# Attention on one core: TensorE's order laid out anew, dummy and bias matmuls taken out, one spare PSUM bank

## The chip, the core and the metric

The kernel runs on one core of one Trainium2 chip. The metric is the device time of one execution in microseconds (us). Executions come in states; where nothing else is said, runs of the same state are compared. Ratios with an interval are the mean time of one kernel's fast runs over that of the other's of the same rounds, so they are not quite the ratio of the medians that are quoted.

## The reference

One attention block in bf16: S = 2048 positions, D = 448, 16 heads of 28.

```
qkv = (x @ wqkv) -> q, k, v            # (16 heads, 2048, 28) each
p   = softmax(q @ k.T * 28 ** -0.5)    # 16 x 2048 x 2048
out = (p @ v, heads side by side) @ wo
```

## The kernel before

The work is cut into 16 units: 4 groups of 4 heads times 4 chunks of 512 queries. A unit has 64 tiles (16 key blocks times 4 heads) of 128 x 512 scores. Most tiles are exponentiated by ScalarE, two or three to an instruction; 109 of the 1024 go to VectorE, which computes the exponential in five instructions. TensorE makes the scores (row-packed, one head in each quarter of the rows), then PV, the product of probabilities and V (column-packed, four heads side by side), the projections of later head groups ("jobs", 38 of them after the start: K, Q and V for one group and one chunk), and the output projection. A block of TensorE writes into a PSUM bank; the instruction that copies it out and frees the bank is its eviction. All orders are static: a list scheduler in the program lays out each engine's instructions from estimated durations.

The parts that the change touches, with cuts marked by "...":

```
LATE0, LATE1 = 1, 8            # units 0 | 1..7 | 8..15 are phases 0 | 1 | 2
def width():                    # ScalarE tiles in one score group
    return ((2, 2), (3, 2), (3, 3))[phase(cur[0])][k % 2]
P.pool("J", [5, 6])             # spare PSUM banks of phases 0 and 1
P.pool("M", [6])                # the spare bank of phase 2
...
def job(...):                   # a projection: 4 TensorE steps, one eviction
    op = P.add("pe", ..., dur=dur, prio=prio, acq=((..."J", 1) if k == 0 else None))
...
def proj_qk(t, g, c, ...):      # K or Q
    if it == 0:                 # constants for VectorE's exponential, in row 28 of each head
        e.matmul(bank(b), CW[:, t, :], ONR[:, :], start=True, stop=False)   # 1 row x 128 columns
    for h in range(4):
        e.matmul(ps[32*h:32*h + DH, ...], w_raw[0:IT, it, col:col + DH], xT[...], start=False, ...)
todo = [(0.85 + (LATE1 - 2.0) * i / len(order),) + o for i, o in enumerate(order)]   # 6.3 jobs a unit
...
# a ScalarE group
s  = P.add("pe", s_mm(... 3 heads ...), dur=330, prio=pr - 5)
ex = P.add("act", exp, ...)
if ph == 2:                     # dummy block: zeros into the open accumulator
    P.add("pe", f_dum, ..., prio=pr + 0.02)
# a VectorE tile: scores of one head, 29 rows
s = P.add("pe", s_mm(... 1 head, DH + 1 rows ...), dur=300, prio=pr - 14/64, acq=("M" or "J", 1))
```

## Time and profile before

| | |
|---|---|
| time, median of 4 runs | 519.11 us (515.7 to 534.44) |
| the profiled run | span 530.0 us, a slow one |
| TensorE, ScalarE, VectorE busy | 92%, 82%, 71% of the span |
| unit 0; units 1 to 6; units 7 to 15; rest | 69.2; 201.6; 242.4; 16.7 us |

From the page of the kernel before: TensorE's busy tenths and its granted clock in 40 slices of the span, then the chain of work that ended last, by engine.

```profile
PE   5999999999999999999999987999799999878884
PEclk9999999985555555555555598557855576999895
...
PE 65%; ACT 31%; DMA 1%; DVE 1%; issue 0%; ACTq 0%
```

TensorE's share of this chain is the largest.

The clock row must be read with care. It shows full clock in the first slices, but the first clock record of this trace is at 87.5 us; before it the row shows 1.0 for want of a record. The timeline of the same kernel (start, duration, engine, line, tile, count), TensorE only:

```profile
30.74 0.61 PE L688 MATMUL ps<-QT,KT 28*128 28x512 bf16 x2
...
31.28 0.61 PE L420 MATMUL ps<-xT,w_raw 112*28 112x512 bf16 x4
...
31.68 0.64 PE L637 MATMUL ps<-PT,V 128*32 128x512 bf16 x4
...
32.25 0.60 PE L688 MATMUL ps<-QT,KT 28*128 28x512 bf16 x2
```

Matmuls packed side by side in the array count as one block. From 31.28 to 31.68 is one column-packed block after another, 0.40 us; from 30.74 to 31.28 there is also a change from row-packed to column-packed, 0.54 us. At half clock over the whole trace a block takes 0.40 to 0.43 us and a change adds 0.10 to 0.14; at full clock a block takes 0.22 us or so and a change adds about 0.10. The start of this run is at half clock.

Windows between the evictions of the accumulator (one a unit; columns: stretch, its length, busy time and count for TensorE, weight loads, VectorE, ScalarE, GpSimd, then granted clock, DMA share, GB/s) for units 3, 7 and 9:

```profile
127.40:164.50 37.10, 37.10 (x250) 9.73 (x247) 27.71 (x50) 28.79 (x25) 0.00 (x0) 0.50 0.04 9
...
270.80:299.70 28.90, 26.08 (x147) 5.07 (x146) 26.41 (x49) 27.88 (x25) 0.00 (x0) 0.50 0.03 11
...
324.60:355.40 30.80, 29.57 (x197) 4.90 (x198) 25.28 (x47) 27.25 (x20) 0.00 (x0) 0.53 0.04 11
```

Unit 3, with projections, is bound by TensorE at half clock: it is busy all of 37.1 us. Unit 7 has no projections and only three dummy blocks, at its end, and is bound by ScalarE. Unit 9 has dummies, and TensorE binds again. The groups that the change removes, from the list by shape:

```profile
L661 PE MATMUL ps<-ZM,ZW 128*32 128x512 bf16 x540 | 65.4, 486 | 0.0
...
L417 PE MATMUL ps<-ONR,CW 1*128 1x512 bf16 x32 | 18.7, 584 | 0.2 <-DMA w_raw<-in_wqkv_dram 0.2
```

### The profile page before, as it was taken

Reading aid. Unit: us, or ns where it says so; the run is one execution under the profiler, and the core shown is the slowest. Engines: PE = TensorE matmul, PEld = TensorE weight load, DVE = VectorE, ACT = ScalarE, POOL = GpSimd, SP = SyncE. Lnnn points to the kernel's source line nnn. Section 1 sums busy time; section 2 is a strip of 40 time slices with the busy share of each in tenths; the row PEclk is TensorE's granted clock in tenths of the full one; section 3 lists DMA queues with packets and bytes.
Section 4 is the critical chain, followed back from the end, with each engine's and each line's share of the span. In section 5 each row is a group of like instructions: output and inputs, shape, how many; then the busy total and the mean of one; then the engine's idle time right before and its main releaser. Section 6 shows DMA issues by size and latency. Waiting matters only on the chain.

```text
span 530.0 us, 8358 instructions
## 1 busy us (share of the span) xinstructions
PE 486.9 (92%) x3557; PEld 118.6 (22%) x3557; DVE 376.8 (71%) x679; ACT 433.9 (82%) x349; POOL 3.9 (1%) x11
## 2 busy tenths in 40 slices
PE   5999999999999999999999987999799999878884
PEld 2442122221222212222111121111111111212131
DVE  2321658996767647666699899879987989594731
ACT  2666678997877768767799999889998999999960
POOL 2000000000000000000000000000000000000000
PEclk9999999985555555555555598557855576999895
DMA  8000000000000000001000000000000000101011
GB/s 258 1 1 0 2 11 15 3 21 2 22 0 3 22 0 23 1 0 23 0 4 20 2 22 3 20 2 22 1 22 1 24 0 24 36 23 36 23 35 41
DMA packets 13843, 10.18 MB, mean 19 GB/s; under 512 B 5932, under 2 KB 11820, under 8 KB 13800
## 3 DMA queue, kind: packets, MB, share of 16 engines
q1 hardware_dynamic: 12872, 8.78, 5.9%
q10 hardware_dynamic: 928, 0.80, 0.5%
q8 instruction: 30, 0.49, 0.4%
q14 instruction: 13, 0.11, 0.1%
HBM read 7.50 MB, written 2.08 MB: 18 GB/s over the span
## 4 chain that ended last, share of the span: by engine, by line
PE 65%; ACT 31%; DMA 1%; DVE 1%; issue 0%; ACTq 0%
ACT PT L700 31%; PE ps L688 26%; PE ps L637 13%; PE ps L420 11%; PE ps L661 6%; PE ps L437 4%; PE ps L417 2%; DMA w_raw<-in_wqkv_dram 1%; PE ps L550 1%; PE ps L401 1%; DVE OTS L573 0%; DVE OUTS L562 0%; PE ps L605 0%; ACT OUTS L560 0%; PE ps L583 0%
## 5 line engine op out<-in xcount | busy, mean ns | idle before, releaser
L700 ACT ACTIVATE PT<-ps 128x1536 bf16<-128x1536 f32 (+1 forms) x343 | 429.7, 1351 | 70.7 <-PE ps L688 67.1
L688 PE MATMUL ps<-QT,KT 28*128 28x512 bf16 (+1 forms) x1024 | 219.2, 532 | 28.9 <-ACT PT L700 26.1
L637 PE MATMUL ps<-PT,V 128*32 128x512 bf16 x915 | 131.9, 540 | 0.0
L718 DVE TENSOR_SCALAR DT<-ps 128x512 int32<-128x512 f32 x109 | 74.7, 685 | 23.6 <-PE ps L688 23.0
L688 PEld LDWEIGHTS ps<-QT,KT 28*128 28x128 bf16 (+1 forms) x1024 | 39.9, 97 | 219.7 <-ACT PT L700 109.2
L722 DVE SCALAR_TENSOR_TENSOR DW<-DW 128x512 f32<-128x512 f32 x109 | 74.2, 683 | 0.9
L724 DVE SCALAR_TENSOR_TENSOR DW<-DW 128x512 f32<-128x512 f32 x109 | 74.1, 682 | 0.4
L726 DVE SCALAR_TENSOR_TENSOR PD<-DT,DW 128x512 int16<-128x512 int32 x109 | 73.5, 677 | 0.8 <-PE ps L637 0.7
L420 PE MATMUL ps<-xT,w_raw 112*28 112x512 bf16 x512 | 65.7, 592 | 0.0
L661 PE MATMUL ps<-ZM,ZW 128*32 128x512 bf16 x540 | 65.4, 486 | 0.0
L637 PE MATMUL ps<-PD,V 128*32 128x512 bf16 x109 | 57.3, 529 | 0.0
L720 DVE TENSOR_SCALAR DW<-DT 128x512 f32<-128x512 uint16 x109 | 45.4, 419 | 0.6
L637 PEld LDWEIGHTS ps<-PT,V 128*32 128x32 bf16 x915 | 26.1, 104 | 49.4 <-issue 44.9
L390 DVE CAST KT<-ps 128x512 bf16<-128x512 f32 x16 | 11.1, 691 | 30.8 <-PE ps L420 30.6
L388 DVE TENSOR_SCALAR QT<-ps 128x512 bf16<-128x512 f32 x15 | 10.3, 688 | 25.2 <-PE ps L420 25.2
L437 PE MATMUL ps<-w_raw,xT 112*128 112x112 bf16 x256 | 28.0, 281 | 0.0
L390 DVE CAST V<-ps 128x448 bf16<-128x448 f32 x16 | 9.9, 622 | 21.0 <-PE ps L437 21.0
L661 PEld LDWEIGHTS ps<-ZM,ZW 128*32 128x32 bf16 x540 | 13.7, 97 | 49.2 <-issue 49.2
L437 PEld LDWEIGHTS ps<-w_raw,xT 112*128 112x128 bf16 x256 | 20.2, 131 | 14.0 <-issue 11.2
L562 DVE CAST OUTS<-ps 128x448 bf16<-128x448 f32 x14 | 8.7, 623 | 20.1 <-PE ps L550 20.1
L550 PE MATMUL ps<-wop,OTN 128*128 128x448 bf16 x64 | 18.5, 406 | 2.4 <-DVE OTN L618 0.8
L420 PEld LDWEIGHTS ps<-xT,w_raw 112*28 112x28 bf16 x512 | 11.7, 107 | 39.4 <-issue 39.1
(44 smaller groups left out, 103.8 us busy)
## 6 DMA issues: line engine op xcount, KB each, us to landing
RB<-scr_r SPq DMA_DIRECT2D x60, 64.0 KB, 2.0
x_nat<-in_x_dram SPq DMA_DIRECT2D x4, 448.0 KB, 7.7
out_dram<-OUTS SPq DMA_DIRECT2D x16, 112.0 KB, 1.7
w_raw<-in_wqkv_dram ACTq DMA_DIRECT2D x2, 392.0 KB, 6.6
w_raw<-in_wqkv_dram SPq DMA_DIRECT2D x1, 392.0 KB, 9.1
wop<-in_wo_dram SPq DMA_DIRECT2D x16, 24.5 KB
scr_l<-OTS SPq DMA_DIRECT2D x15, 8.0 KB
LT<-scr_l SPq DMA_DIRECT2D x15, 8.0 KB, 1.6
```

The source lines that it names most:

```text
L420: ins = e.matmul(ps[32 * h:32 * h + DH, b * 512:(b + 1) * 512], w_raw[0:IT, it, col:col + DH], xT[0:IT, it, c * 512:(c + 1) * 512], start= ...
L437: ins = e.matmul(ps[:, b * 512 + j * GD:b * 512 + (j + 1) * GD], xT[0:IT, it, n * 128:(n + 1) * 128], w_raw[0:IT, it, 2 * D + g * GD:2 * D ...
L550: return e.matmul(bank(hold[0].banks[0])[:, 0:D], OTN[:, gg, n * 128:(n + 1) * 128], wop[:, gg, :], start=(gg == 0), stop=(gg == G - 1))
L637: ins = e.matmul(ps[32 * h:32 * h + 32, ACC * 512:(ACC + 1) * 512], V[:, kt, hh * 32:(hh + 1) * 32], p_ap, start=(kt == 0), stop=(kt == NK ...
L661: ins = e.matmul(ps[32 * h:32 * h + 32, ACC * 512:(ACC + 1) * 512], ZW[:, :], ZM[:, :], start=False, stop=False, skip_group_check=True, ti ...
L688: ins = e.matmul(bank(b), KT[32 * h:32 * h + rows, g, kt * 128:(kt + 1) * 128], QT[32 * h:32 * h + rows, g, c * QCH:(c + 1) * QCH], start= ...
L700: ex = P.add("act", (lambda e, p0=p0, w=w, b0=b0: e.activation(PT[:, p0 * 512:(p0 + w) * 512], bank(b0, w), AF.Exp, scale=ESCALE)), deps=[ ...
L718: o1 = P.add("dve", (lambda e, T=T, s=s: e.tensor_scalar(T, bank(s.banks[0]), 0.0, 255.0 * 65536.0 - 1.0, ALU.max, ALU.min)), deps=[s, d_l ...
L720: o2 = P.add("dve", (lambda e, F16=F16, W=W: e.tensor_scalar(W, F16, ES, EC, ALU.mult, ALU.add)), deps=[o1, d_last[di]], dur=360, prio=pr, ...
L722: o3 = P.add("dve", (lambda e, W=W: e.scalar_tensor_tensor(W, W, EA, W, ALU.add, ALU.mult)), deps=[o2], dur=610, prio=pr, name=f"D3_{gi}")
L724: o4 = P.add("dve", (lambda e, W=W: e.scalar_tensor_tensor(W, W, EB, W, ALU.add, ALU.mult)), deps=[o3], dur=610, prio=pr, name=f"D4_{gi}")
L726: o5 = P.add("dve", (lambda e, W=W, T=T, pi=pi: e.scalar_tensor_tensor(PD[:, pi, :], T, 1.0 / 512.0, W, ALU.mult, ALU.add)), deps=[o4, slo ...
```

## The change

The intent: since TensorE runs at half clock most of the time, lay its order out for that. In parts:

- **Dummies** (540 matmuls, units 8 to 15) go.
- **Bias rows** go. The constants of VectorE's exponential move into its own arithmetic.
- **Riding**: the scores of a VectorE tile are to follow a score group of the three other heads at once, so that all four run together.
- **One spare bank and groups of three** from unit 1 on (from unit 8 on before).
- **Jobs**: at 4.1 a unit by priority instead of 6.3; once begun a job isn't interrupted (priority -4), and its eviction goes first on VectorE.
- **Layout**: the scheduler's durations for TensorE are those of half clock after 45 us, with a price for a change of packing.

```
-    LATE0, LATE1 = 1, 8
+    LATE0, LATE1 = 1, 1
+    def pe_dur(self, prev, op, t):
+        one, switch = (220.0, 100.0) if t < self.FULL_CLOCK_UNTIL else (430.0, 110.0)
+        if prev is None or prev.kind != op.kind:
+            return switch + one * op.units
+        if op.kind == "r" and op.heads and not set(op.heads) & set(prev.heads):
+            return 60.0
+        return one * op.units
...
 def job(...):
-                           dur=dur, prio=prio, ...
+                           kind=kind, units=units_, prio=prio if (k == 0 or early) else -4.0, ...
-            ev = P.add(evac_eng, fe, ..., prio=prio, ...)
+            ev = P.add(evac_eng, fe, ..., prio=prio if early else -100.0, ...)
...
-                    if it == 0:
-                        e.matmul(bank(b), CW[:, t, :], ONR[:, :], start=True, stop=False)
-            todo = [(0.85 + (LATE1 - 2.0) * i / len(order),) + o ...]
+            todo = [(0.85 + i / 4.1,) + o ...]
...
-                if ph == 2:
-                    P.add("pe", f_dum, deps=[ms_zw, ms_zm], after=[s], dur=300, ...)
...
-                s = P.add("pe", ..., deps=deps, dur=300, prio=pr, ...)
+                for j in range(idx[0] - 1 - DLEAD, ..., -1):
+                    if j in s_of and (j - idx[0] + 1) % 4 == 0:
+                        partner, p_pr = s_of[j]
+                        break
+                s = P.add("pe", ..., deps=deps, after=[partner], kind="r", ..., prio=p_pr + 0.0001, ...)
...
+        P.FULL_CLOCK_UNTIL = 45000.0
```

The rule for which tiles go to VectorE changes a little too (114 instead of 109). The diff has two more edits: VectorE's first step of a tile, which frees the spare bank, goes ahead of its other work (priority -90), and K and Q blocks write 32 instead of 28 columns a head.

More of the change, by code (lines that the diff above doesn't have):

```diff
@@ L20 @@
     __slots__ = ("eng", "emit", "deps", "after", "dur", "prio", "name", "idx", "sig", "count",
-                 "t0", "t1", "dma_group", "dma_index", "acq", "rel", "banks", "slack", "nbytes", "relpool", "acq_slack")
+                 "t0", "t1", "dma_group", "dma_index", "acq", "rel", "banks", "slack", "nbytes", "relpool", "acq_slack", "kind", "units", "heads")
     def __init__(self, eng, emit, deps, after, dur, prio, name, idx, dma_group):
@@ L44, in __init__ @@
         self.acq_slack = 0.0
+        self.kind = None
+        self.units = 0.0
+        self.heads = ()
 class _DmaGroup:
@@ L63 @@
     BIGLOOK = 150.0
+    FULL_CLOCK_UNTIL = 0.0
     def __init__(self):
@@ L71, in pool, with add @@
         self.pools[name] = {b: [0.0, None, False] for b in banks}
-    def add(self, eng, emit, deps=(), after=(), dur=100.0, prio=0.0, name="", dma_group=None, acq=None, rel=(), slack=0.0, nbytes=0, acq_slack=0.0):
+    def add(self, eng, emit, deps=(), after=(), dur=100.0, prio=0.0, name="", dma_group=None, acq=None, rel=(), slack=0.0, nbytes=0, acq_slack=0.0, kind=None, units=1.0, heads=()):
         assert dma_group is not None or eng != "sp"
@@ L82, in add @@
         op.acq_slack = acq_slack
+        op.kind = kind
+        op.units = units
+        op.heads = heads
         self.ops.append(op)
         return op
+    def pe_dur(self, prev, op, t):
+        if op.kind is None:
+            return op.dur
+        one, switch = (220.0, 100.0) if t < self.FULL_CLOCK_UNTIL else (430.0, 110.0)
[4 more added lines that the diff above has]
+        return one * op.units
     def schedule(self):
@@ L145, in schedule @@
             op.t0 = st
+            if e == "pe":
+                op.dur = self.pe_dur(order[e][-1] if order[e] else None, op, st)
             op.t1 = st + op.dur
@@ L236 @@
 LOG2E = 1.4426950408889634
-ES = 1.3267265379831447e-05
-EC = 0.0001429470584999315
-EA = 6.764643559880514
-EB = -6.640897709782045
+ES = 3.285997142359445e-05
+EC = 27.848949706562973
+EA = -77.30729786983042
+EB = 1961.0831047043987
+ZLO = -127.0 * 65536.0
+ZHI = 128.0 * 65536.0 - 1.0
 def _fast(nc, x, wqkv, wo, out, n_heads=16):
@@ L265, in _fast @@
     VONE = DH
-    CROW = DH
     QSCALE = 65536.0 * LOG2E * scale
     ESCALE = 1.0 / (65536.0 * LOG2E)
-    KCONST = 127.0
-    QCONST = 3.671875
     assert DH * H == D and G * 4 == H and DH + 1 <= 32 and NIT * IT == D and GD <= IT
@@ L296, in _fast @@
         DW = sb("DW", [128, NDB, 512], FP32)
-        CW = sb("CW", [1, 2, 128], BF16)
-        ONR = sb("ONR", [1, 512], BF16)
+        DU = sb("DU", [128, NDB, 512], FP32)
         OTS = sb("OTS", [128, 2, 512], FP32)
@@ L349, in _fast @@
         ms_wop = P.add("pool", lambda e: e.memset(i32v(wop.rearrange("p g d -> p (g d)")), 0), dur=900, prio=-8, name="ms_wop")
-        CW4 = CW.rearrange("p t (h r) -> p t h r", r=32)
-        ms_c0 = P.add("dve", lambda e: e.memset(CW[:, :, :], 0.0), dur=100, prio=-11, name="ms_c0")
-        ms_cq = P.add("dve", lambda e: e.memset(CW4[:, 0, :, CROW], QCONST), deps=[ms_c0], dur=100, prio=-11, name="ms_cq")
-        ms_ck = P.add("dve", lambda e: e.memset(CW4[:, 1, :, CROW], KCONST), deps=[ms_c0], dur=100, prio=-11, name="ms_ck")
-        ms_onr = P.add("dve", lambda e: e.memset(ONR[:, :], 1.0), dur=100, prio=-11, name="ms_onr")
         ms_one = P.add("pool", lambda e: e.memset(ONE[:, :], 1.0), dur=100, prio=-7, name="ms_one")
@@ L372, in _fast @@
         mid_ev = []
+        cur_pool = ["J"]
         def job(name, prio, mm_ops, evac, early, evac_eng="dve", evac_dur=610, after=(), mul=None):
@@ L377, in job @@
             prev = None
-            for k, (f, deps, dur) in enumerate(mm_ops):
+            pool = "E" if early else cur_pool[0]
+            for k, (f, deps, kind, units_) in enumerate(mm_ops):
                 op = P.add("pe", (lambda e, f=f: f(e, hold[0].banks[0])),
-                           deps=list(deps) + (list(early_ev) if (k == 0 and not early) else []), after=[prev] + list(after),
-                           dur=dur, prio=prio, name=f"{name}_{k}", acq=(("E" if early else "J", 1) if k == 0 else None), acq_slack=0.0 if early else ASLACK)
+                           deps=list(deps) + (list(mid_ev if pool == "M" else early_ev) if (k == 0 and not early) else []), after=[prev] + list(after),
+                           kind=kind, units=units_, prio=prio if (k == 0 or early) else -4.0, name=f"{name}_{k}", acq=((pool, 1) if k == 0 else None), acq_slack=0.0 if early else ASLACK)
                 if k == 0:
@@ L390, in job @@
                 fe = (lambda e: e.tensor_copy(evac[0](), evac[1](hold[0].banks[0])))
-            ev = P.add(evac_eng, fe, deps=[prev] + list(evac[2:]), dur=evac_dur, prio=prio, name=f"{name}_ev", rel=[(hold[0], 0)])
-            (early_ev if early else mid_ev).append(ev)
+            ev = P.add(evac_eng, fe, deps=[prev] + list(evac[2:]), dur=evac_dur, prio=prio if early else -100.0, name=f"{name}_ev", rel=[(hold[0], 0)])
+            if pool != "M":
+                (early_ev if early else mid_ev).append(ev)
             return ev
@@ L403, in f @@
                 return ins
-            xt_ev[(it, n0 // 4)] = job(f"xT{it}_{n0}", prio, [(f, [id_b_op, dma_x[n0 // 4]], 300)],
+            xt_ev[(it, n0 // 4)] = job(f"xT{it}_{n0}", prio, [(f, [id_b_op, dma_x[n0 // 4]], "f", 1.1)],
                                        ((lambda: xT[0:IT, it, n0 * 128:(n0 + 4) * 128]), (lambda b: bank_bf(b)[0:IT, 0:512])),
@@ L415, in f @@
                     ins = None
-                    if it == 0:
-                        e.matmul(bank(b), CW[:, t, :], ONR[:, :], start=True, stop=False)
                     for h in range(4):
                         col = t * D + g * GD + h * DH
-                        ins = e.matmul(ps[32 * h:32 * h + DH, b * 512:(b + 1) * 512], w_raw[0:IT, it, col:col + DH],
-                                       xT[0:IT, it, c * 512:(c + 1) * 512], start=False, stop=(it == NIT - 1), tile_position=(0, 32 * h))
+                        ins = e.matmul(ps[32 * h:32 * h + 32, b * 512:(b + 1) * 512], w_raw[0:IT, it, col:col + 32],
+                                       xT[0:IT, it, c * 512:(c + 1) * 512], start=(it == 0), stop=(it == NIT - 1), tile_position=(0, 32 * h))
                     return ins
-                mms.append((f, [xt_ev[(it, c)]] + ([dma_w[t], ms_cq, ms_ck, ms_onr] if it == 0 else []), 540 if it == 0 else 290))
+                mms.append((f, [xt_ev[(it, c)]] + ([dma_w[t]] if it == 0 else []), "c", 1.0))
             kq_ev[(t, g, c)] = job(f"p{t}_{g}_{c}", prio, mms,
@@ L439, in f @@
                     return ins
-                mms.append((f, [xt_ev[(it, c)] for it in range(NIT)] + [dma_w[2]], 300))
+                mms.append((f, [xt_ev[(it, c)] for it in range(NIT)] + [dma_w[2]], "f", 1.1))
             Vd = V[:, 4 * c:4 * c + 4, g * 128:(g + 1) * 128].rearrange("p n (h r) -> p n h r", r=32)[:, :, :, 0:DH]
@@ L464, in late_jobs, with make_late @@
                 order += [("q", g, c) for c in range(1, NCH)]
-            todo = [(0.85 + (LATE1 - 2.0) * i / len(order),) + o for i, o in enumerate(order)]
-            for pr, kind, g, c in sorted(todo):
+            todo = [(0.85 + i / 4.1,) + o for i, o in enumerate(order)]
+            return sorted(todo)
+        def make_late(jobs):
+            for pr, kind, g, c in jobs:
                 if kind == "v":
@@ L470, in late_jobs @@
                     proj_qk(1 if kind == "k" else 0, g, c, pr, False)
-            return [t[0] for t in todo]
-        late_units = [min(max(int(pr), 0), NU - 1) for pr in late_jobs()]
+        todo_late = late_jobs()
+        late_units = [min(max(int(t[0]), 0), NU - 1) for t in todo_late]
+        make_late([t for t in todo_late if t[0] < LATE1 - 0.25])
         tiles = [(u, kt, h) for u in range(NU) for kt in range(NK) for h in range(4)]
@@ L483, in _fast @@
         on_dve = set()
+        run = 0
         for i, (u, kt, h) in enumerate(tiles):
             if i % 64 == 0:
-                t_d = max(t_d, t_a) + dve_load[u]
-            if t_d + DCOST <= t_a + LEAD and i < NT - 12:
-                t_d = max(t_d, t_a - 2.0) + DCOST
+                t_d += dve_load[u]
+            if t_d + DCOST <= t_a + LEAD and i < NT - 12 and run % (2 if u < LATE0 else 3) == 0:
+                run = 0
+                t_d = max(t_d, t_a - 6.0) + DCOST
                 on_dve.add(i)
@@ L491, in _fast @@
                 t_a += ACOST
+                run += 1
         items = []
@@ L552, in out_proj @@
                 opm = P.add("pe", f_op, deps=[otn_ev[(gg, cc)]] + mid_ev + (([otn_ev[(g_, cc)] for g_ in range(G)] + dma_wo[-1:]) if gg == 0 else []),
-                            after=[prev], dur=260, prio=pr, name=f"OP{n}_{gg}", acq=(("M", 1) if gg == 0 else None), acq_slack=ASLACK)
+                            after=[prev], kind="f", units=0.9, prio=pr if gg == 0 else -4.0, name=f"OP{n}_{gg}", acq=(("M", 1) if gg == 0 else None), acq_slack=ASLACK)
                 prev = opm
@@ L631, in f_pv @@
                 ins = None
-                acc_open[0] = kt != NK - 1
                 for h in range(4):
@@ L641, in pv @@
                        + [v_ev[(g, kt // 4)]] + ([acc_ev[0]] if kt == 0 else []),
-                       after=[last_pv[0]], dur=320, prio=u + (kt + 4) / NK, name=f"PV{u}_{kt}", slack=1200.0 if kt == 0 else 0.0)
+                       after=[last_pv[0]], kind="c", units=1.0, prio=u + (kt + 4) / NK, name=f"PV{u}_{kt}", slack=1200.0 if kt == 0 else 0.0)
             last_pv[0] = op
@@ L650, in _fast @@
         pv_next = 0
-        acc_open = [False]
-        ZW = sb("ZW", [128, 32], BF16)
-        ZM = sb("ZM", [128, 512], BF16)
-        ms_zw = P.add("pool", lambda e: e.memset(ZW[:, :], 0.0), dur=100, prio=-4, name="ms_zw")
-        ms_zm = P.add("pool", lambda e: e.memset(ZM[:, :], 0.0), dur=300, prio=-4, name="ms_zm")
-        def f_dum(e):
-            ins = None
-            if acc_open[0]:
-                for h in range(4):
-                    ins = e.matmul(ps[32 * h:32 * h + 32, ACC * 512:(ACC + 1) * 512], ZW[:, :], ZM[:, :],
-                                   start=False, stop=False, skip_group_check=True, tile_position=(0, 32 * h))
-            return ins
+        s_of = {}
+        DLEAD = 12
         nd = 0
@@ L675, in _fast @@
             ph = phase(idx[0])
+            if ph == 2 and cur_pool[0] != "M":
+                cur_pool[0] = "M"
+                make_late([t for t in todo_late if t[0] >= LATE1 - 0.25])
             if ph > 0 or kind == "D":
@@ L680, in _fast @@
             pr = idx[0] / 64.0 - 0.2
-            rows = DH if kind == "A" else DH + 1
             hold = []
@@ L697, in _fast @@
                 s = P.add("pe", (lambda e, tl=tl, b0=b0: s_mm(e, tl, range(b0, b0 + 3), DH)), deps=deps, after=[last_s[0]],
-                          dur=330, prio=pr - 5, name=f"S{gi}")
+                          kind="r", units=1.0, heads=tuple(h for _, _, h in tl), prio=pr - 5, name=f"S{gi}")
                 last_s[0] = s
+                s_of[idx[-1]] = (s, pr - 5)
                 ex = P.add("act", (lambda e, p0=p0, w=w, b0=b0: e.activation(PT[:, p0 * 512:(p0 + w) * 512], bank(b0, w), AF.Exp, scale=ESCALE)),
@@ L702, in _fast @@
                 last_exp[0] = ex
-                if ph == 2:
-                    P.add("pe", f_dum, deps=[ms_zw, ms_zm], after=[s], dur=300, prio=pr + 0.02, name=f"DUM{gi}")
                 for j, t in enumerate(tl):
@@ L709, in _fast @@
             else:
-                pr -= 14 / 64.0
+                partner, p_pr = None, pr - 14 / 64.0
+                for j in range(idx[0] - 1 - DLEAD, max(idx[0] - 1 - DLEAD - 32, 0), -1):
+                    if j in s_of and (j - idx[0] + 1) % 4 == 0:
+                        partner, p_pr = s_of[j]
+                        break
                 di, pi = nd % NDB, nd % NPD
                 nd += 1
-                s = P.add("pe", (lambda e, tl=tl, hold=hold: s_mm(e, tl, [hold[0].banks[0]], DH + 1)), deps=deps,
-                          dur=300, prio=pr, name=f"SD{gi}", acq=("M" if ph == 2 else "J", 1), acq_slack=ASLACK)
+                s = P.add("pe", (lambda e, tl=tl, hold=hold: s_mm(e, tl, [hold[0].banks[0]], DH)), deps=deps, after=[partner],
+                          kind="r", units=1.0, heads=(tl[0][2],), prio=p_pr + 0.0001, name=f"SD{gi}", acq=("M" if ph == 2 else "J", 1), acq_slack=ASLACK)
@@ L715, in _fast @@
                 hold.append(s)
-                T, W = DT[:, di, :], DW[:, di, :]
+                T, W, U = DT[:, di, :], DW[:, di, :], DU[:, di, :]
                 F16 = DT[:, di, :].bitcast(U16).rearrange("p (n two) -> p n two", two=2)[:, :, 0]
-                o1 = P.add("dve", (lambda e, T=T, s=s: e.tensor_scalar(T, bank(s.banks[0]), 0.0, 255.0 * 65536.0 - 1.0, ALU.max, ALU.min)),
-                           deps=[s, d_last[di]], dur=610, prio=pr, name=f"D1_{gi}", rel=[(s, 0)])
+                o1 = P.add("dve", (lambda e, T=T, s=s: e.tensor_scalar(T, bank(s.banks[0]), ZLO, ZHI, ALU.max, ALU.min)),
+                           deps=[s, d_last[di]], dur=610, prio=-90.0, name=f"D1_{gi}", rel=[(s, 0)])
@@ L720, in _fast @@
                 o2 = P.add("dve", (lambda e, F16=F16, W=W: e.tensor_scalar(W, F16, ES, EC, ALU.mult, ALU.add)),
                            deps=[o1, d_last[di]], dur=360, prio=pr, name=f"D2_{gi}")
-                o3 = P.add("dve", (lambda e, W=W: e.scalar_tensor_tensor(W, W, EA, W, ALU.add, ALU.mult)),
+                o3 = P.add("dve", (lambda e, W=W, U=U: e.scalar_tensor_tensor(U, W, EA, W, ALU.add, ALU.mult)),
                            deps=[o2], dur=610, prio=pr, name=f"D3_{gi}")
-                o4 = P.add("dve", (lambda e, W=W: e.scalar_tensor_tensor(W, W, EB, W, ALU.add, ALU.mult)),
+                o4 = P.add("dve", (lambda e, W=W, U=U: e.scalar_tensor_tensor(U, U, EB, W, ALU.add, ALU.mult)),
@@ L725, in _fast @@
                            deps=[o3], dur=610, prio=pr, name=f"D4_{gi}")
-                o5 = P.add("dve", (lambda e, W=W, T=T, pi=pi: e.scalar_tensor_tensor(PD[:, pi, :], T, 1.0 / 512.0, W, ALU.mult, ALU.add)),
+                o5 = P.add("dve", (lambda e, U=U, T=T, pi=pi: e.scalar_tensor_tensor(PD[:, pi, :], T, 1.0 / 512.0, U, ALU.mult, ALU.add)),
                            deps=[o4, slot_last.get(("D", pi))], dur=610, prio=pr, name=f"D5_{gi}")
```

## The prediction

> **What bounds the kernel now.** TensorE in most of the span, ScalarE's exponentials in the rest: the chain of waits that ended last is 65% TensorE, 31% ScalarE. By stage (windows between the accumulator evictions to OTS): unit 0 ends at 69.2 us; units 1 to 6 take 29.2, 29.0, 37.1, 35.1, 39.0, 32.2 us; units 7 to 14 take 24 to 25 us where the granted clock is mostly full and 30.7 where it is half; the tail takes 16.7 us. The profiled run is a slow one (530; median 518).
>
> The clock lane overstates the clock: its first record is at 87.5 us, yet from 10 to 85 us the timeline shows blocks of four packed matmuls 0.43 us apart, as in the half-clock stages (0.23 to 0.33 at full clock). So TensorE is at half clock before 87.5 us, and from 115 to 306 us. The Trainium skill (TensorE: Matmul & The Clock Gate, "Back-to-back issue gap") gives N/1.2 ns at half clock, 427 ns for 512 columns: the trace agrees. Going from a row-packed block to a column-packed one costs 0.10 us more in the timeline (0.96 us for two blocks and the change); the skill (TensorEngine Tiling (Array Packing), "Key Properties") says that a mode change drains.
>
> A half-clock unit in phase 2 is then 19 score blocks, 8 separate VectorE-tile score blocks, 19 dummy blocks, 16 PV blocks, 62 x 0.43, plus 38 changes x 0.11: 30.9 us; 30.7 measured.
>
> **What the change does**
> - Dummies go (540 matmuls, 135 blocks of 0.43 us at half clock): critical only where the clock is half in units 8 to 15.
> - Bias rows go: 32 matmuls with their mode changes, about 0.54 us each; 6 in unit 0.
> - VectorE-tile scores ride. By the diff's rule for the tile lists, of 114 such tiles (109 before) 65 have a partner group that already holds their head and still cost 0.43; about 46 cost 0.06. Saving 15 to 20 us of TensorE time.
> - Groups of three from unit 1 on: 19 instead of 23 groups per unit, 4 x (0.43 + 0.2) us less on TensorE in units 1 to 7; ScalarE 0.449 us per tile instead of 0.46.
> - Projections spread over units 1 to 9, about 4 jobs per unit instead of 6 to 7, 1.75 us each, uninterrupted; one spare bank serves VectorE tiles, projections and output projections.
>
> **After, per unit at half clock.** Without projections: (19 + 16) x 0.43 + 2 + 4 = 21 us TensorE, below ScalarE's 57 x 0.449 = 25.6. With 4 jobs: 28.5 TensorE; an uninterrupted job delays the next scores, costing ScalarE 0.4 to 1.1 us. VectorE needs about 24.7. All three are near balance: I expect 28.7 us in units 1 to 9 and 26 to 27.5 in units 10 to 14.
>
> Sum: 65.5 + 9 x 28.7 + 5 x 26.5 + 23.5 + 16 = 496; full-clock spells take off a few: 494 us, range 480 to 510. Faster by over 2%: 0.8; within: 0.18; slower: 0.02.
>
> **Right if** no unit takes over 31 us, ScalarE's exponentials take over half of the chain, no ZM/ZW group remains, half clock covers more of the span and matters less, and runs scatter less. **Wrong if** the single spare bank binds (score blocks waiting on VectorE's DT eviction or on copies of K, Q, V), if VectorE's tiles arrive late at PV, or if the clock without dummies behaves differently (much more full clock: 475 to 480).

## More of the kernel before

ScalarE waited 67 us in all for scores (who waited for whom: us in total, times, longest):

```profile
ACT PT L700 <- PE ps L688: 67.1, 96, 2.2
```

## The result, and the profile after

| | before | after |
|---|---|---|
| median of 4 runs | 519.11 us | 470.55 us (458.68 to 481.83) |
| ratio of the fast runs | | 0.8887, 95% interval 0.8812 to 0.8961 |

The kernel is faster by 11%, the prediction said 5%. (Five later rounds on another chip gave 0.8988, so 10%.) The runs of the kernel after are of two kinds: 458.7, 460.5 and 461.8 us, and 479.3 and 481.8. The median lies between them; no run took it. The profile is of the second kind. A later run of the same kernel, unchanged, gave a profile of the first kind (`a_same5` below). Slow beside slow, 530.0 against 477.6; the fast profile has 460.9. The clock row and the chain, first of the profile, then of the fast one:

```profile
PEclk9655555566565657777555758555667756575985
...
ACT 41%; PE 40%; DVE 12%; DMA 4%; issue 2%; SPq 0%; ACTq 0%
```

```profile
PEclk9999556756756577675658695555757555567795
...
ACT 52%; PE 32%; DVE 11%; DMA 2%; issue 1%; SPq 0%
```

ScalarE now leads the chain (31% before), and waits for scores 26 us in all instead of 67 (13 in the fast profile):

```profile
ACT PT L711 <- PE ps L698: 26.1, 54, 1.4
PEld ps L698 <- DVE DT L731: 25.5, 47, 1.1
```

The second line shows the one bank: weight loads for scores that wait until VectorE's DT step frees it (7.3 us in the kernel before). Such idle time is not by itself a loss. VectorE's share of the chain rose from 1% to 12%. The two kinds differ at the start: in the slow one the trace has full clock for one spell of 3.4 us at 11.5 us, then half clock to 104 us; in the fast one full clock from 10.4 to 48 us. Unit 0, first of the slow profile, then of the fast one followed by units 3, 8, 10 and 15:

```profile
0.00:61.50 61.50, 53.48 (x380) 19.38 (x380) 19.81 (x37) 37.65 (x38) 3.43 (x9) 0.62 0.20 55
```

```profile
0.00:44.00 44.00, 35.40 (x380) 15.18 (x380) 19.42 (x38) 34.18 (x38) 3.43 (x9) 1.00 0.26 77
...
99.10:127.00 27.90, 22.76 (x182) 6.94 (x180) 24.25 (x45) 27.18 (x21) 0.00 (x0) 0.68 0.06 12
...
231.60:259.40 27.80, 24.45 (x197) 6.58 (x194) 26.62 (x47) 26.70 (x21) 0.00 (x0) 0.68 0.05 12
...
281.80:306.30 24.50, 22.82 (x145) 5.58 (x143) 24.49 (x47) 24.33 (x19) 0.00 (x0) 0.50 0.04 12
...
415.20:444.10 28.90, 24.37 (x154) 6.85 (x151) 14.18 (x27) 21.45 (x17) 0.00 (x0) 0.80 0.15 50
```

Unit 0 is 17.5 us shorter with the fast start, which is the whole difference between the two profiles (16.7 us). In units 3, 8 and 10 ScalarE is busy over 95% of the time, in unit 10 at a clock of 0.50. Unit 15 is long: in it, ScalarE is busy 21.5 of 28.9 us while output projections run.

Where the time went, with the blocks counted from the starts of the matmuls in both slow traces:

| units 1 to 6 | before | after |
|---|---|---|
| score blocks / PV blocks / K,Q blocks / bias blocks | 164 / 96 / 96 / 24 | 172 / 96 / 48 / 0 |
| V matmuls (about 0.10 us) | 192 | 80 |
| changes of packing (mode changes) | 302 | 169 |
| sum at half clock: blocks x 0.43 + V x 0.10 + changes x 0.11 | 216 us | 162 us |
| measured; ScalarE busy | 201.6; 159.9 us | 162.2; 156.8 us |

The half-clock sum is an estimate from durations of these traces. It fell by 54 us: 32 for jobs moved away, 10 for the bias, 15 for the changes, and 3 back for more score blocks. It counts the bias too dear: of the 24 bias blocks 16 follow a score block without the cost of a change (0.40 us from start to start), and 7 of these start within 0.1 us of it and cost nothing; some 5 of the 216 us are not there. The rest of the gap to 201.6 is in line with the 27 us of full clock from 87.5 us on. The time fell by 39 us, to where ScalarE stands. In units 7 to 15 the 135 dummy blocks went and half of the jobs came: 242.4 to 236.3 us. So most of the gain, 39 of 52 us, lies in units 1 to 6. Riding hardly took place: score blocks are 436 before and 444 after in the whole trace, and in the slow trace after only 19 blocks have four matmuls (12 before). The timeline of the fast profile after, TensorE only, shows why:

```profile
118.64 0.39 PE L698 MATMUL ps<-QT,KT 28*128 28x512 bf16 x3 [0.87 <-ACT PT L711]
118.96 0.40 PE L657 MATMUL ps<-PT,V 128*32 128x512 bf16 x4
119.30 0.39 PE L698 MATMUL ps<-QT,KT 28*128 28x512 bf16 x1
119.98 0.39 PE L698 MATMUL ps<-QT,KT 28*128 28x512 bf16 x3 [0.30 <-ACT PT L711]
...
122.25 0.81 PE L698 MATMUL ps<-QT,KT 28*128 28x512 bf16 x4
```

At 119.30 a VectorE tile's score stands alone, after PV; at 122.25 four matmuls in a row take 0.81 us, not the 0.39 of one block: they didn't all run together. The first started at 122.25, when a DT step had freed the bank, the other three at 122.67. By the order of TensorE's instructions, 81 of the 114 follow a PV block. By the scheduler's own times (its order made again from the kernel), the one spare bank, for which they wait, is still held when the partner's score block ends in 79 of the 114, mostly by the VectorE tile before.

### The profile page after: what moved, and what is told of

Same layout as the page of the kernel before. It is cut to its first block, busy times and chain, and to the rows that moved or that the text cites. A ratio compares the mean times of both kernels' runs of the same rounds, so it can differ in the third digit from the quotient of the medians.

```text
span 477.6 us, 7257 instructions
## 1 busy us (share of the span) xinstructions
PE 418.7 (88%) x2985; PEld 113.1 (24%) x2985; DVE 387.9 (81%) x700; ACT 419.8 (88%) x321; POOL 3.4 (1%) x9
## 4 chain that ended last, share of the span: by engine, by line
ACT 41%; PE 40%; DVE 12%; DMA 4%; issue 2%; SPq 0%; ACTq 0%
ACT PT L711 41%; PE ps L698 16%; PE ps L657 8%; PE ps L434 8%; PE ps L451 4%; PE ps L571 3%; DVE DT L731 3%; DVE DU L737 2%; DVE PD L739 2%; DMA w_raw<-in_wqkv_dram 2%; DMA RB<-scr_r 1%; DVE DU L735 1%; PE ps L417 1%; DVE DW L733 1%; DVE OTS L594 1%
## 5 line engine op out<-in xcount | busy, mean ns | idle before, releaser
L711 ACT ACTIVATE PT<-ps 128x1536 bf16<-128x1536 f32 (+1 forms) x315 | 415.6, 1447 | 28.9 <-PE ps L698 26.1
L698 PE MATMUL ps<-QT,KT 28*128 28x512 bf16 x1024 | 208.3, 549 | 42.3 <-ACT PT L711 35.5
L698 PEld LDWEIGHTS ps<-QT,KT 28*128 28x128 bf16 x1024 | 40.2, 97 | 209.8 <-ACT PT L711 129.8
L735 DVE SCALAR_TENSOR_TENSOR DU<-DW 128x512 f32<-128x512 f32 x114 | 77.7, 685 | 0.6
L739 DVE SCALAR_TENSOR_TENSOR PD<-DT,DU 128x512 int16<-128x512 int32 x114 | 77.5, 682 | 0.2
L737 DVE SCALAR_TENSOR_TENSOR DU<-DU,DW 128x512 f32<-128x512 f32 x114 | 77.4, 682 | 0.2
L657 PE MATMUL ps<-PD,V 128*32 128x512 bf16 x114 | 61.6, 543 | 0.0
L434 PE MATMUL ps<-xT,w_raw 112*32 112x512 bf16 x512 | 54.7, 556 | 1.9 <-DVE DT L731 0.8
L434 PEld LDWEIGHTS ps<-xT,w_raw 112*32 112x32 bf16 x512 | 14.6, 120 | 27.0 <-issue 16.4
L657 PEld LDWEIGHTS ps<-PD,V 128*32 128x32 bf16 x114 | 11.4, 101 | 8.9 <-issue 8.9
```

The lines of the kernel that those rows point to most:

```text
L434: ins = e.matmul(ps[32 * h:32 * h + 32, b * 512:(b + 1) * 512], w_raw[0:IT, it, col:col + 32], xT[0:IT, it, c * 512:(c + 1) * 512], start= ...
L657: ins = e.matmul(ps[32 * h:32 * h + 32, ACC * 512:(ACC + 1) * 512], V[:, kt, hh * 32:(hh + 1) * 32], p_ap, start=(kt == 0), stop=(kt == NK ...
L698: ins = e.matmul(bank(b), KT[32 * h:32 * h + rows, g, kt * 128:(kt + 1) * 128], QT[32 * h:32 * h + rows, g, c * QCH:(c + 1) * QCH], start= ...
L711: ex = P.add("act", (lambda e, p0=p0, w=w, b0=b0: e.activation(PT[:, p0 * 512:(p0 + w) * 512], bank(b0, w), AF.Exp, scale=ESCALE)), deps=[ ...
L735: o3 = P.add("dve", (lambda e, W=W, U=U: e.scalar_tensor_tensor(U, W, EA, W, ALU.add, ALU.mult)), deps=[o2], dur=610, prio=pr, name=f"D3_{ ...
L737: o4 = P.add("dve", (lambda e, W=W, U=U: e.scalar_tensor_tensor(U, U, EB, W, ALU.add, ALU.mult)), deps=[o3], dur=610, prio=pr, name=f"D4_{ ...
```

## The experiments

The theory going in (W): what was gained is TensorE work at half clock, removed or moved from where TensorE binds. Rivals: the clock itself changed because the dummies went (C); the layout is the gain, not the amount or place of the work (L). All 18 runs gave correct results. "The kernel after" stands for 458 to 463 us with the fast start and 479 to 482 with the slow one. Each run came with new runs of the kernel before; their fast mean was 501.6 to 512.5 us by chip.

### Dummies taken out of the kernel before (b_nodum)

```
-                if ph == 2:
+                if False:
                     P.add("pe", f_dum, ...
```

> The kernel before without its 135 dummy blocks in units 8 to 15, nothing else changed. Theory W (the gain is TensorE work removed where TensorE binds at half clock): only the units of 8 to 15 that ran at half clock gain, about 5 us each (30.7 to about 26), units 1 to 6 stay at 29 to 39 us: 10 to 20 us in all, ratio 0.96 to 0.98. Rival C (the dummies held the granted clock down or shaped it; without them full-clock spells come often and the whole kernel speeds up): ratio under 0.95 and a higher mean clock in units 8 to 15. If the dummies did their work of holding the clock up, the ratio is over 1.0.

Measured: 499.3 to 508.2 us, median 505.3, beside 515.4 (507.2 to 535.1). Units 7 to 15 took 232 us instead of 242, at a clock of 0.50 in six of the nine; units 1 to 6 stayed at 27 to 37 us. That is what W expects; C falls as far as the kernel before goes. The dummies cost about 10 us in half-clock units.

### Dummies put back (a_dum, a_dumfix)

In `a_dum` the dummy is added as before, for units from 8 on, and the scheduler lays out everything anew.

> The kernel after with the dummy block put back behind every score group of units 8 to 15. Theory W: at half clock such a unit needs 21 + 19 x 0.43 = 29 us of TensorE, so it takes 29 to 31 us instead of 26: 15 to 30 us more than the kernel after, ratio to before 0.92 to 0.95. If full clock comes oftener by the dummies, less: 0.89 to 0.91. Units 1 to 7 unchanged (24 to 28 us) in both.

Measured: 515.7 to 536.3, ratio 1.008. This miss says little of dummies. The new order held the jobs back and put 13 of them into unit 8, which took 48.4 us. `a_dumfix` puts the dummy into the finished order, so nothing else moves (shortened):

```
+        for op in P.order["pe"]:
+            if due and not op.name.startswith("SD"):
+                new.append(dummy); due = False
+            new.append(op)
+            due = due or op in dum_after      # score groups of units 8 to 15
```

> The kernel after with a dummy block behind every score group of units 8 to 15, put into the finished order so that nothing else moves (the earlier try let the jobs pile up in unit 8). At half clock a unit of 8 to 13 then needs 21 + 19 x 0.43 + 1 + 2.7 x 1.8 = 35 us of TensorE. Theory W2 (the dummies had filled the slack in which projections now lie): 20 to 45 us more than the kernel after, ratio 0.93 to 0.97. If dummies cost nothing because they bring full clock: under 0.905.

Measured: 461.0, 465.1, 465.4 with the fast start, 480.2 and 481.5 with the slow one: at most 4 us more than the kernel after. The clock row shows why the expected 20 to 45 us aren't there:

```profile
PEclk9999999996566657577557999659997989897899
```

(Its first record is at 104 us, so the first slices again say nothing.) Units 8 to 15 ran at a clock of 0.62 to 1.00, 0.88 in the mean; the whole trace has 208 us of full clock against 109 in the slow profile after. In the fast runs the mean clock on record is 0.77 to 0.78, against 0.67 to 0.69 in those of the kernel after. So the dummies' own time is about paid by the clock that comes with them. That they had filled slack which the projections needed (W2) asked for 20 to 45 us; the loss isn't there.

### Where the jobs lie (a_conc, a_conc2, a_even, a_noride)

> The kernel after, with the projection jobs at 6.3 to a unit in units 1 to 6 as before, instead of 4.1 in units 1 to 9. Theory W: units 1 to 6 need 21 + 6.3 x 1.8 = 32 us of TensorE at half clock instead of 28.5, units 7 to 9 fall to 25.6: 10 to 18 us more than the kernel after, ratio 0.91 to 0.925. If the spreading doesn't matter: 0.885 to 0.895.

`a_conc` changes the rate of the jobs' priorities back to 6.3 a unit. Measured: 469.4 and 474.9, 486.7 and 488.5. The edit didn't do what it was meant to: TensorE's order still has 1 to 4 jobs in each of units 1 to 9, then 6 each in units 10 and 11 and the last in 12. The priority doesn't decide; VectorE tiles' scores beat every job to the one spare bank. But units 10 and 11 are a test of the sum: expected for 6 to 6.5 jobs up to 21 + 6.5 x 1.8 = 32.7 us at half clock, measured 32.8 and 33.7 at a clock of 0.53 and 0.59.

`a_conc2` lets the jobs win the bank:

```
-   prio=prio if (k == 0 or early) else -4.0
+   prio=(prio if early else prio - 5.6) if (k == 0 or early) else -4.0
-   0.85 + i / 4.1
+   0.85 + 6.0 * i / len(order)
```

> The kernel after with its 38 late projection jobs really in units 1 to 6 (7, 7, 6, 6, 6, 3 by TensorE's order, as before; in the kernel after it is 2 to 5 in each of units 1 to 12). Theory W2 (the gain is projections moved out of TensorE-bound units into the slack that the dummies had filled): units 1 to 5 take about 21 + 6.5 x 1.8 = 32 us at half clock, less in full-clock spells, units 7 to 12 about 25.5: 10 to 25 us more than the kernel after, ratio 0.91 to 0.94. Rival L (the layout, whole jobs and fewer mode changes, is the gain, not where the jobs lie; this order has 495 mode changes, as few as the kernel after): ratio 0.885 to 0.90.

Measured: 471.2 to 476.2, all with the fast start: 13 us more than the kernel after. Its units 1 to 4:

```profile
43.30:81.90 38.60, 33.41 (x282) 10.03 (x282) 27.56 (x49) 36.22 (x27) 0.00 (x0) 0.69 0.05 11
81.90:112.80 30.90, 27.46 (x225) 8.04 (x225) 25.07 (x45) 26.39 (x21) 0.00 (x0) 0.67 0.04 10
112.80:143.80 31.00, 26.57 (x232) 7.84 (x232) 27.15 (x48) 27.30 (x21) 0.00 (x0) 0.72 0.04 11
143.80:176.00 32.20, 26.35 (x241) 7.51 (x240) 26.08 (x45) 26.19 (x19) 0.00 (x0) 0.73 0.03 9
```

Units 1 to 6 took 190.5 us against 161.8 in the fast profile after, units 7 to 15 221.6 against 238.3. Crowding costs more than it returns.

`a_even` spreads jobs 3 to 4 a unit and starts output projections earlier (rate 3.2, priorities 5.2 and 6.5 lower).

> A try at a better version: the kernel after with jobs 3 to 4 a unit through unit 12 (3, 4, 3, 3, 3, 5, 3, 3, 4, 2, 3, 1) and output projections 4 each in units 13 and 14 instead of 0 and 3. By theory W2 no unit is over 27 us and unit 15 falls from 28.2 to about 23: 4 to 8 us less than the kernel after, ratio 0.875 to 0.885. If ScalarE's 25.6 us bound was already everywhere the limit: same as the kernel after.

Measured: 460.8 and 462.3, 479.4 and 480.4: the same as the kernel after. Unit 15 did fall to 21.7 us, but units 2, 6, 9 and 13 took 28.8 to 31.0. The time is not lost in one place that can be smoothed.

`a_noride` undoes the partners (the loop over partners is empty), which gives the VectorE tiles' scores their older priority.

> The kernel after without partners for the VectorE tiles' scores: their priority is the older, lower one. In both orders only 35 to 38 of 114 such blocks stand beside a score block without their head, and the trace of the kernel after shows only 19 that ran together with three others, so riding saves nothing: expected from that alone is the kernel after's time, 460 with a fast start, 480 with a slow one. But the lower priority lets the jobs have the bank earlier, 4 a unit in units 1 to 9, as the prediction had assumed: if what counts is where jobs lie, units 1 to 9 take 28 to 29 us instead of 26.5 and the time is 5 to 15 us longer. If riding was worth its 15 to 20 us of TensorE work, also longer, but with more score blocks in the trace (over 460 instead of 444).

Measured: 468.2 and 468.8, 489.0 and 491.7: 8 to 10 us more. Score blocks in the trace: 435, not more than the 436 and 444 of the two profiles after. So riding, as written, saves nothing. But the order now has 4 or 5 jobs in each of units 1 to 9, as the prediction had assumed, and those took 28.5 us in the mean, where the prediction said 28.7. Units 4 and 5:

```profile
126.50:158.80 32.30, 30.68 (x219) 7.76 (x219) 30.62 (x55) 29.95 (x23) 0.00 (x0) 0.58 0.04 10
158.80:190.70 31.90, 29.27 (x202) 8.34 (x202) 27.16 (x47) 30.45 (x23) 0.00 (x0) 0.58 0.04 10
```

### Whole jobs and the layout (a_split, a_fullmodel)

`a_split` gives the later steps of a job the job's own priority.

> The kernel after, with the later matmuls of a projection job at the job's own priority again, so that score groups may come between them (TensorE's order has 548 mode changes instead of 502). Theory W: 46 changes x 0.12 us, about 5 us more, ratio 0.89 to 0.905. If keeping jobs whole is the main thing in units 1 to 9 (the bank is held longer when they are split): 10 us or more, ratio over 0.91. If uninterrupted jobs cost ScalarE, as the prediction had it (0.4 to 1.1 us a job): faster than the kernel after, under 0.885.

Measured: 482.0, 496.9, 502.4 and 503.5; the profiled 496.9 had the slow start. That is 15 us or more over the kernel after, start for start. The new order also left all 16 output projections to unit 15 and beyond and put 6 jobs each into units 8 and 12 (33.4 and 34.9 us), so the cost of splitting by itself stays unmeasured.

`a_fullmodel` tells the scheduler that the clock is full throughout (`P.FULL_CLOCK_UNTIL = 1e12`).

> The kernel after, its order laid out by the scheduler for full clock throughout (220 ns a block instead of 430). The order has 568 mode changes instead of 502; jobs lie 2 to 4 to a unit in units 1 to 12. Theory W: 66 changes x 0.11 us, 7 us, and misplaced blocks cost ScalarE: 8 to 20 us more than the kernel after. If the layout for half clock is not the gain: within 4 us of it, start for start.

Measured: 473.7 to 476.9, the profile with the fast start: 15 us more. The work is the same but for 66 more changes of packing, about 7 us at half clock. The rest, put down to placing, is not separated from the clock: the trace has 123 us of full clock against 143 in the fast profile after. Undoing the layout costs 15 us; which part of it is not shown.

### The bias (a_biasfix, a_bias128, a_biaswarm)

`a_biasfix` puts a zero bias back, one row deep, with the scheduler's durations left alone so that the order stays.

```
+                    if it == 0:
+                        e.matmul(bank(b), CW[:, t, :], ONR[:, :], start=True, stop=False)   # CW zeros, ONR ones
```

> The kernel after with a zero bias matmul (one row, 128 columns, as before) put back ahead of each of the 32 K and Q jobs, TensorE's order otherwise the same. It adds 0.43 us and a mode change, 0.54 us, at half clock: 17 us of TensorE work in all. Theory W: only TensorE-bound stretches feel it, unit 0 (6 of them, 2 to 3 us) and part of the rest: 3 to 10 us more than the kernel after, ratio 0.895 to 0.91. If all of TensorE's work counts: 17 us, ratio 0.92.

Measured: 497.2 to 504.9, some 40 us over the kernel after. The profile has the slow start (unit 0 65.0 us). Against the slow profile after it is 17.8 us more, near the 17 of "all of TensorE's work counts"; the rest is the start. In this order most bias blocks follow a PV block, where one adds 0.67 us at half clock (1.07 us from PV to K/Q block, 0.40 without it); in the kernel before most followed a score block and added 0.42 us or nothing. So putting the bias back costs more than the kernel before paid for it. `a_bias128` has the same instructions with 128 rows of zeros and ones.

> The bias put back as in the run with zero bias rows, but 128 rows deep (zeros against ones) instead of one row; TensorE's order and the count of blocks the same. Theory A (the granted clock follows how much of the array is active; a one-row block costs 0.43 us and a mode change without earning clock, a 128-row block earns what it costs, as the dummies did): the kernel falls back towards the kernel after, 462 to 470 us with a fast start, 480 to 488 with a slow one, mean clock over 0.66, and both starts occur. Theory B (a bias block costs its time, 17 us, whatever its rows): 495 to 505 us, or 478 to 482 with a fast start, mean clock about 0.63.

Measured: 473.6 to 477.8, and the profile has the fast start (unit 0 45.9 us): 15 us over the fast kernel after. The clock rows, first of one row, then of 128:

```profile
PEclk9999955555556555568555859555555755565895
```

```profile
PEclk9999656676666569875555767555555656575999
```

(In the first the earliest record is at 58.5 us.) The two programs differ in nothing but the rows, but ran on different chips. (The second trace lacks 23 of its 32 bias matmuls; the gaps show that they ran.) Neither theory holds whole: behind a PV block a bias block costs the same whatever its rows (1.07 us in both), as B said; behind a score block the 128-row one takes 1.07 us too, the one-row one 0.54 or 0.95. And the one-row kernel had the slow start or its times in every run, the 128-row one in none; why is not shown. `a_biaswarm` is the one-row version with the warm start of the next section.

> The kernel after with the one-row zero bias put back and the 18 zero blocks ahead. If a bias block costs its own time at half clock, whatever the start: 473 to 480 us, 15 to 18 more than the warm kernel, as the 128-row bias did with a fast start; the other 20 us of the 40 were the start. If the one-row bias also costs granted clock later on: 485 us or more, and a mean clock under 0.63.

Measured: 475.4, 479.4, 483.2 and 485.2, the fast runs 477.4 in the mean against 458.4 for the warm kernel on the same chip: 19 us. Units 1 to 6 took 9.6 us more than in the warm kernel's profile, for 12 bias blocks and 22 changes, 7.6 us by the sum; full clock is 99 us against 154. The profiled run is one of the two slow ones, though its unit 0 had the fast start. Over all four runs the mean clock is 0.59 to 0.64, over six of the warm kernel 0.67 to 0.70. So the one-row bias costs its own time and a little clock.

### The start (a_warm, a_same5, a_warm5, b_warm)

Eighteen zero blocks on TensorE, into the accumulator's bank, while it waits for the first loads:

```
+        for i_ in range(NWARM):        # 18
+            warm = P.add("pe", f_warm, deps=[ms_zw, ms_zm], after=[warm], dur=1.0, prio=-50)
```

> A try at a better version: the kernel after with 18 zero blocks of four column-packed matmuls on TensorE before its first work, while it waits for the first loads. Runs of the kernel after fall into two kinds, 459 to 462 us with full clock from about 10 to 45 us and unit 0 of 43 us, and 479 to 482 us with half clock there and unit 0 of 61 us. If the kind is decided by TensorE being busy in the first 10 us, all runs take 456 to 463 us. If not: both kinds still occur.

Measured: 456.8 to 460.5, all four of the fast kind. Then five rounds beside the kernel after itself:

> The kernel after, unchanged, beside the next one on the same chip. Expected: two kinds of runs, 458 to 463 and 478 to 483 us, each in a third to two thirds of the runs.

> The kernel after with 18 zero blocks on TensorE ahead of its first work, as in the run with the warm start, in five rounds. If the warm start decides the kind: all runs 456 to 463 us, none at 478 to 483, so about 10 us less in the mean than the unchanged kernel. If the four fast runs before were luck: both kinds again.

Measured: the kernel after 459.8 to 462.7, ratio 0.8988 (0.8942 to 0.9034); warm 455.0 to 460.4, ratio 0.8935 (0.8875 to 0.8995). Here the kernel after had the fast start in six of six, so the expected two kinds didn't show, and the gain of the warm start is 2.7 us in the mean. In the profiles that gain isn't in unit 0 (43.8 against 44.0 us) but in the tail: 14.1 against 16.8 us, at a clock of 0.93 against 0.60. Over all, warm runs are fast in ten of ten, those of the kernel after in nine of eleven. That the warm start decides the kind is likely, not shown.

> The kernel before with the same 18 zero blocks ahead, order otherwise the same. If the kernel before has the same two starts: all its runs in the lower part of its spread, 500 to 512 us, none at 518 to 539, so part of the gain of the change in the medians is the start. If its spread comes from the clock in later units: unchanged, 507 to 530.

Measured: 513.1 to 519.4, 1.1% over the fast runs of before. Neither expectation holds: its unit 0 took 47.9 us at full clock, as the first said, but all four runs lie above its 512, and two of them, at 519.3 and 519.4, where none should. Units 1 to 6 took 204.5 us, as in the slow profile before (201.6). Against the warm kernel after, start for start, the difference is 511.3 to 458.5 us in the profiles, 41 of it in units 1 to 6. So most of the gain of the change isn't the start.

### One bank, and riding made real (a_late8, a_merge)

`a_late8` sets LATE1 back to 8: groups of three and two and two spare banks in units 1 to 7.

> The kernel after with groups of three and two and two spare banks in units 1 to 7 again, as before. By TensorE's order the jobs then come earlier (5, 8, 9, 3 in units 1 to 4, 9 more in units 7 to 9) and there are 26 more score groups. If the one spare bank is what spreads the projections: units 1 to 3 take 30 to 36 us at half clock, and the kernel 10 to 25 us more than the kernel after, 470 to 485 with a fast start. If two banks relieve a wait for the bank: the same or faster, 455 to 462.

Measured: 473.0 to 475.7 and one of 494.0: 13 us more. With two banks the jobs crowd into units 1 to 4 (32.5, 28.4, 30.2, 30.4 us). The edit also brings 26 more score groups, but the trace has 429 score blocks, no more than that of the kernel after. The loss in the profile, 10 us, lies in units 1 to 6 (171.8 against 161.8 us), where the jobs are. So two banks are no gain here: the one bank holds the jobs apart. What waits for it cost by themselves is not measured.

`a_merge` puts the VectorE tile's matmul into the TensorE step of its partner, which then takes the bank (shortened):

```
+    s.emit = lambda e: (s_mm(e, ptl, range(pb0, pb0 + 3), DH), s_mm(e, tl, [s.banks[0]], DH))[1]
+    s.acq = ("M", 1)
```

> The kernel after with riding enforced: groups aligned so that none spans a VectorE tile, and the VectorE tile's score matmul put into the same TensorE step as the three of its partner from unit 2 on (106 of 115), which waits for the spare bank. About 100 of the 444 score blocks should go (43 us at half clock), and the trace should show some 100 blocks of four. If TensorE work is what counts: 440 to 450 us. If the partner's wait for the one spare bank costs ScalarE as much or more, or the jobs, pressed into units 1 to 6 in this order, cost it: over 470.

Measured: 490.2 to 492.3 and one of 508.3, 30 us more. Riding took place: 110 blocks of four and 328 score blocks instead of 436 in `a_same5`. But the waits (engine and line, what it waited for, us in total, times, longest), first of this run, then of the fast profile after:

```profile
ACT PT L715 <- PE ps L701: 46.0, 48, 2.4
...
PE ps L701 <- DVE DT L741: 17.9, 20, 1.5
```

```profile
ACT PT L711 <- PE ps L698: 13.0, 30, 1.1
```

ScalarE waits 33 us more for scores that wait for the bank or for their turn, and units 2 to 6 take 30 to 35 us with TensorE busy only 22 to 25. Its order also has 5 to 7 jobs in each of units 2 to 6, so not all of it is the bank. With one spare bank, real riding is no gain here.

## Why the prediction was wrong

It said 494 us, 480 to 510; the median is 470.55. Faster was right, the size was less than half of what came.

- **The base of the sum.** The profiled run of before was known to be a slow one (530 us), yet the sum was built on its unit 0 at half clock and then set against the median of 518. "65.5" for unit 0 was 61.5 with the slow start and 44 with the fast one. Start for start the forecast of 496 stands against 477.6, so 18 us are wrong in the sum. The rest is the start: the median is that of two fast and two slow runs, which the prediction didn't foresee.
- **"I expect 28.7 us in units 1 to 9."** This is the term that failed: 26.5 in the slow profile, nine times 2.2 us, 19.5 us. The price was right: with 4 or 5 jobs a unit (`a_noride`) it was 28.5. The number of jobs was wrong. "About 4 jobs per unit" was read from the priorities; in the order that was made it is 2 to 4 in units 1 to 9 (26 of the 38), with the rest as late as unit 14. The list scheduler gives the bank to VectorE's tiles first. ScalarE's own term, 25.6 us a unit, was right: it was busy 230.5 us in the nine units. So TensorE's 28.5 was not the bound that the prediction took it for.
- **"VectorE-tile scores ride ... saving 15 to 20 us"**: none. The check of heads was right as far as it went, but the bank, still held in 79 of 114 by the scheduler's times, keeps most from following their partner: 436 score blocks before, 444 after.
- **"Bias rows ... about 0.54 us each"**: 17 us by that; 15 to 19 measured at the same start by putting it back, which overstates what the kernel before paid (above).
- **"Dummies go"**, critical only at half clock in units 8 to 15: 10 us in the kernel before, at most 4 in the kernel after. Right in kind.
- **"An uninterrupted job ... costing ScalarE 0.4 to 1.1 us"**: with 26 jobs in units 1 to 9 of the slow profile, ScalarE was idle 8.4 us in all, 0.3 us a job, at most. Mis-sized, the second reason for 26.5.
- **Changes of packing** were counted for a unit without jobs only. In units 1 to 6 they fell from 302 to 169, 15 us; the layout (`a_fullmodel`, 15 us) was not in the sum.
- **Units 10 to 14** at 26.5: 26.3. **Unit 15** at 23.5: 28.2, since 13 of the 16 output projections were left to it and the tail.
- **What would show it right**: ScalarE leads the chain (41 and 52%) and no ZM/ZW group remains, as said. "Over half" holds for the fast profile only. "No unit over 31": unit 11 takes 31.7, with 4 jobs. "Runs scatter less": no, 23 us against 19. "Wrong if the single spare bank binds": in part it did, 25 us of weight loads waiting for DT, but ScalarE waited less than before, and how much time that cost is open. "Wrong if ... much more full clock: 475 to 480": the slow runs came near that time, but not by this; the slow trace has less full clock, 109 against 140 us recorded.

What the single undoings cost (13 for the places of the jobs, 15 for the layout, 15 to 19 for the bias, 13 for the bank and groups) is not to be added up: by the account above each pushes TensorE above the same ScalarE bound. How a unit's order decides whether the clock rises is open.

The version with the warm start has the lowest time: 459.1 us median in five rounds, 0.6% in the mean under the kernel after on the same chip, with overlapping intervals, and no run of the slow kind in ten.

## What to carry to other kernels

Where one engine's load per stage lies near another's, what a change removes counts only in the stages where that engine binds: sum each stage's blocks with the durations of its own clock, and count the jobs in the order that was really made, not in the priorities. Check the granted clock by the spacing of equal instructions, above all before the first clock record, and compare runs of the same start. A trick of overlap that needs a buffer (here a fourth head that needs the one spare bank) is to be looked for in the trace before it is credited.

## What the Trainium skill lacked or had wrong

- TensorE: Matmul & The Clock Gate, "What's actually happening", has full clock come after one busy window of about 3.4 us. Busy was not enough here: in units 3 to 5 of the kernel before TensorE was busy 110.7 of 111.2 us by the profile and stayed at half clock, which lasted 191 us on end. The window itself agrees: full-clock spells after are 3.4, 6.8, 10.2, 13.7 and 20.5 us.
- The same page doesn't say how much of the array's rows work must use to earn the clock. Dummies of 128 rows put into an unchanged order raised full clock from 109 to 208 us of the trace (both slow starts). One-row bias blocks kept full clock to 99 us, against 154 without them (both warm starts); 128-row ones left it at 157 us, against 143 without (both fast starts).
- The same page, "Seeing it yourself", warns that clock records can't be fully trusted; it doesn't say that a profile shows full clock before the first record. Here that was 87.5 us with blocks 0.40 to 0.43 us apart.
- TensorEngine Tiling (Array Packing), "Key Properties", says that a change of mode drains the array, without a figure: 0.10 to 0.14 us at half clock here, some 290 times in units 1 to 6 of the kernel before (302 changes by kind, of which those from a score to a one-row bias block cost none).
